# DeltaNet and a multiplicative FFN in one hand-ordered kernel: a new list of steps behind the 130th

## The chip, the cores and the metric

The kernel runs on one core of one Trainium2 chip. The metric is the device time of one execution in microseconds (us), lower is better. The time before is a median of three runs. Engines are named as the profile names them: PE is TensorE's matmul, PEld its weight load, DVE is VectorE, ACT is ScalarE, POOL is GpSimd, SP is SyncE, which issues nearly all DMAs.

## What is computed

```python
# q, k, v: (4, 8, 768, 48), beta: (4, 8, 768); all float32
k_n = k / (np.linalg.norm(k, axis=-1, keepdims=True) + 1e-06)
for t in range(S):
    y[:, :, t] = np.einsum('bhd,bhde->bhe', q[:, :, t], state)
    v_old = np.einsum('bhde,bhd->bhe', state, kt)
    state = state + bt[:, :, :, None] * np.einsum('bhd,bhe->bhde', kt, vt - v_old)
x = y.transpose(0, 2, 1, 3).reshape(3072, 384)
a, b = x @ w1, x @ w2          # w1, w2: (384, 1024), float64 inputs
out = ((a * b) @ w3) @ w_out   # w3: (1024, 1024), w_out: (1024, 384)
```

The first part is a delta-rule attention over 768 tokens for 32 pairs of batch and head; the second is an FFN whose two branches are multiplied elementwise. The four weights arrive as float64 and are converted on the chip.

## The kernel before

**The work.** The 768 tokens are cut into 12 chunks of 64. For each chunk the kernel builds triangular score matrices, inverts them (two chunks together) and runs a short chain that updates the state; from the chain's results it makes the transposed attention output xT. The FFN works on units of two chunks (u = 0 to 5). w3 and w_out are multiplied together once, ahead of all units ("folds"), so that a unit needs a product with w1, one with w2, the elementwise product, and one product with the folded weight. Strassen-like sums of weights and tokens save some of the products.

**The order.** Each piece of work is a Python generator, and each `yield` ends a step. A string, ORDER, lists 1,458 steps by name; the kernel walks through it and lets the named generator make its next step. The same name stands in the list as often as it has steps. Afterwards every engine's instructions are chained in exactly this order:

```python
for name in ORDER.split():
    step(name)
in_text_order()      # each instruction behind the one before it on its engine
```

So the list fixes, for each engine, what stands behind what; an engine whose next instruction waits does nothing else. Between engines only data and buffers decide.

**Buffers that matter.** `in_turn(pool, shape, tag, n, ...)` hands out n buffers in rotation, in the order of the list. The two PSUM pools are psF with four single banks (tag "f": transposes, folds and FFN products) and psW with two pairs of banks (tag "w": scores, corners, chains, outputs). An inverse that lives in PSUM keeps ("holds") one of the two pairs from its first copy to its last, and all others then share the other pair:

```python
V = two_banks().rearrange("p a (s t) -> p (a s) t", t=BS)
held.add(("w", turns["w"]))
```

**The steps.** In this document "t4#2" is the second time that t4 stands in the list, which is its second step.

- P0 to P35: a piece of a weight. #1 DMA issues (SP, L791), #2 ACT (L799, L800), #3 DVE (L802, L803), #4 POOL (L807). P0 to P7 are w_out, P8 to P23 w3, P24 to P29 w1, P30 to P35 w2.
- t0 to t15: transpose of a w3 piece. #1 PE (L842) into a bank of psF, #2 ACT copy (L845).
- f0 to f7: fold. #1 and #2 PE (L856), #3 ACT (L863).
- g0 to g5: squares of k; POOL products (L285) and DVE reductions (L287) alternate (for g1: #1, #3, #5, #7 POOL, #2, #4, #6, #8 DVE), then ACT. N0 to N5: norms, on DVE.
- p, d: load q and k permuted (SP), transpose them on DVE (L339).
- s0 to s11: scores. #1 PE (L383, L389), #2 DVE (L395), #3 the masked part (DVE L413 in chunks 2 and 3); then the second half likewise.
- u, V0 to V5: layout for the inverse, and the inverse. V1#1 sets a buffer on POOL, V1#2 transposes on DVE, V1#3 and #4 copy into PSUM on ACT (L475), V1#5 to #35 are 31 pairs of DVE instructions (L484, L489; L495, L500 in other forms), V1#36 transposes back.
- e0 to e11: corner of the inverse; in chunks 0 to 3: #1 and #3 ACT (L549), #2 POOL, #4 DVE, #5 PE (L576), #6 ACT (L601), #7 PE (L576), #8 ACT (L621).
- c0 to c11: chain. For c1 and later: #1 PE, #2 DVE, #3 PE, #4 DVE (L687), #5 PE, #6 DVE; c0 starts with what is #3 there. y0 to y11: outputs. #1 PE (L746), #2 ACT into xT (L767), #3 DMAs of 16 rows of xT.
- b and a00 to a07: FFN products of unit 0 (PE L876). a, h, i, j with two digits: those of the later units (PE L995). T, W, S, G: sums of weights and tokens on POOL. o, x: the last product (PE L1105) and the results.

Of the kernel before, what the change touches and what calls it, by code (L numbers as in the profile page):

```python
# [40 lines left out]
beta K0 K0 K0 k1 K1 P10 P11 P12 P3 P12 g0 g0 Q0 P10 g0 g0 g0 g0 g0 P8 Q0 Q0 Q0 K1 K1 K1 Q0 K1 P3  # L41
N0 P9 k2 P8 P8 P10 s0 P8 N0 g1 s0 s0 s0 s0 s0 s0 u0 q1 P2 Q1 P9 p2 P2 P12 P12 P9 Q1 g1 Q1 Q1 P2
u0 g1 Q1 d2 d2 u0 P5 P1 t0 t0 t5 t5 P9 t2 t2 P4 P6 s1 s1 P5 P5 P2 s1 P1 s1 s1 s1 u1 g1 P1 u1 u1
t4 V0 V0 P5 V0 V0 P4 t10 P7 P4 t3 t3 V0 V0 P1 f1 P6 P6 t4 V0 P7 V0 V0 t10 t1 P14 P7 P4 V0 f0 V0
P6 P16 P16 V0 V0 P7 t1 s0 P19 P19 P19 P19 V0 f1 P17 k3 p2 v1 V0 V0 P14 P14 P14 V0 f2 P17 f2 f0 V0
f2 P15 v0 P20 f1 t11 f0 P17 P17 f5 V0 V0 P16 t11 P16 t8 P15 V1 V0 t8 f5 t9 V0 V0 t6 P15 V0 n0 n0
f5 V0 V0 V0 V0 t9 P20 P20 V0 t6 P22 P22 P22 f4 P23 P23 V0 f4 f4 P21 P21 P15 t7 t7 V0 s1 V0 V0 V0
V0 g1 d2 d2 P22 f3 f3 P24 P20 g1 g1 p3 g1 P26 p3 P30 e0 e0 e0 t12 t14 e1 e1 g1 f3 e0 e0 d3 d3 N1
s2 s2 s2 P23 P23 t12 e0 f6 e0 p4 s2 P24 e1 e1 t14 s2 e0 P24 s2 P25 c0 P26 f7 u2 P30 P24 c0 e1 e1
P21 P21 d3 d3 y0 y0 P26 P26 P31 t15 t13 s3 s3 s3 s3 s3 s3 t13 c0 n1 n1 P32 t15 u2 u2 u3 c0 P30 f7  # L50
e1 P25 P25 P31 P31 P27 c1 c1 u3 u3 f6 e1 c1 V1 V1 V1 y0 P31 f6 f7 P25 P27 V1 V1 V1 V1 P30 b1 c1
N1 b1 v2 P32 V1 V1 P27 V1 s1 y1 y1 b2 V1 d4 V1 V1 P28 P29 P32 b2 P27 V2 V1 V1 V1 y1 b3 V1 V1 P28
P28 b0 P32 c1 b2 b2 b3 b1 b1 b0 P29 P29 b0 P29 a03 a03 a02 V1 b0 V1 d4 V1 V1 a01 V1 P28 V1 V1 a02
V1 P35 a01 a00 a00 n2 n2 a04 a04 b7 P33 P33 a05 a05 P34 P34 a01 a07 b7 V1 b4 b5 V1 V1 V1 V1 k4
a01 a07 k5 b5 b3 g2 b4 V1 V1 P35 V1 V1 g2 c1 e2 e2 e2 e2 a06 a06 g2 e3 e3 e3 b3 g2 g2 a00 a02 a02
p4 v3 d4 d4 p5 a00 e2 P34 c2 c2 e2 P34 e2 b6 P35 P35 e2 c2 c2 e3 a03 g2 g2 P33 b6 y2 g2 P33 g2 d5
d5 p5 c2 c2 y2 a04 e3 s4 N2 e3 s4 a03 s4 b6 b6 s4 s4 s4 s4 T e3 T T d5 n3 d5 a04 e3 b4 b4 b7 s5
n3 k6 g3 u4 s5 s5 s5 s5 s5 s5 b5 b7 b5 a05 T c3 c3 a06 a05 a06 u5 V2 p6 g3 a07 a07 c3 c3 g3 S0 S0
S0 V2 g3 V2 V2 N2 oD0 y3 y3 V2 V2 W oA0 S0 S0 V2 V2 S0 S0 S0 c3 v5 n5 V2 V2 S0 S0 S0 S0 V2 v4 oB0
V2 V2 V2 xA0 V2 V2 xB0 V2 V2 oA0 S0 S0 S0 n4 oB0 xA0 d6 y3 k7 xA0 V2 n4 oC0 V2 V2 V2 a10 xB0 S0  # L60
V2 V2 xC0 G1 V2 xD0 a10 a10 V2 oC0 a10 a10 d6 xC0 xC0 xC0 xD0 V2 V2 i10 V2 h10 c3 c4 V2 V2 j10 V2
V2 V2 a10 h10 i10 a12 V2 V2 h10 W W a12 p6 V2 a12 a12 j12 e4 g3 g3 h10 c4 a12 h10 a12 h12 d6 d6
s5 i12 e4 e4 e4 i10 h12 h12 g3 g3 p7 g3 e4 e4 h12 N3 s4 h12 a11 a11 a11 s6 s6 i12 i12 e5 c4 j11
s6 c4 y4 y4 c4 e5 d7 d7 h11 c4 c5 a11 p7 e5 s6 a11 a11 h11 i11 i11 n5 c5 d7 d7 N3 a13 h11 h11 e5
W e5 s7 e5 a13 s7 s7 s7 s7 s7 s7 a13 a13 s6 s6 c5 i11 k8 u7 u6 g4 g4 g4 S1 V3 V3 c5 p8 h11 s6 g4
h13 a13 j13 a13 i13 h13 i13 i13 S1 h13 V3 h13 h13 V3 V3 y5 V3 V3 V3 V3 V3 V3 d8 V3 V3 V3 y5 oC1
oA1 S1 oD1 S1 S1 V3 V3 S1 xA1 c5 oA1 xA1 oB1 v6 y5 v7 a20 a20 V3 xA1 V3 V3 V3 d8 G2 V3 V3 xB1 n6
V3 V3 V3 V3 oB1 xB1 xC1 S1 j20 k9 V3 xD1 V3 V3 V3 V3 S1 oC1 a20 a20 p8 xC1 V3 xC1 h20 V3 xD1 xC1
V3 V3 V3 V3 a20 a20 i20 h20 a22 h20 g4 c5 g4 g4 g4 a22 V3 j22 d8 h20 h20 e6 i20 g4 a22 d8 a22 h22
a22 a22 i22 e6 V4 e6 c6 i20 h22 e6 i22 h22 n7 h22 e6 e6 a21 a21 a21 n6 c6 p9 c6 s8 i22 N4 h21 h22  # L70
i21 a21 s8 a21 s6 c6 y6 s8 s8 j21 s8 v8 a21 h21 i21 y6 d9 d9 e7 p9 e7 s8 s8 e7 e7 s7 h21 h21 i21
h21 a23 c6 c6 e7 a23 i23 a23 n8 n8 d9 e7 S2 N4 d9 a23 s9 s9 s9 s9 s9 n7 s9 k10 s9 u8 g5 a23 a23
c7 c7 h23 h23 i23 i23 c7 c7 g5 u9 h23 h23 V4 V4 V4 j23 h23 S2 g5 g5 V4 V4 V4 V4 p10 v9 V4 y7 y7
V4 V4 oA2 V4 V4 d10 V4 y7 V4 V4 S2 oD2 S2 d10 xA2 V4 S2 S2 oB2 oC2 V4 c7 xB2 V4 V4 V4 V4 oB2 xB2
xC2 xD2 p10 V4 V4 V4 oA2 V4 V4 a30 a30 G3 a30 a30 S2 S2 oC2 k11 V4 xC2 j30 s9 V4 xD2 xC2 V4 V4 V4
V4 V4 V4 xA2 xA2 xC2 g5 a30 h30 a30 i30 a32 h30 V4 V4 V4 e8 h30 i30 c7 a32 j32 h30 h30 g5 a32 a32
i32 g5 g5 d10 d10 i30 a32 a32 e8 h32 h32 i32 p11 e8 e8 a31 a31 c8 e8 s8 c8 g5 a31 j31 e8 c8 n9 c8
h32 h32 h32 y8 y8 c8 e9 e9 i31 d11 d11 h31 e9 e9 n9 a31 c8 s10 a31 p11 i32 N5 s10 s10 a31 h31 s10
s10 s10 s10 c9 c9 h31 e9 e9 d11 d11 u10 i31 i31 s11 a33 a33 S3 a33 v11 h31 h31 s11 s11 s11 s11
s11 a33 c9 i33 a33 a33 c9 h33 h33 s11 u11 i33 i33 j33 h33 h33 V5 V5 V5 V5 y9 S3 h33 V5 V5 V5 v10  # L80
n10 n10 oA3 S3 S3 V5 V5 oD3 V5 oB3 s10 y9 y9 oC3 V5 V5 S3 S3 V5 V5 V5 V5 V5 xA3 xB3 V5 V5 n11 V5
V5 oB3 V5 xB3 xD3 xC3 xC3 xD3 oA3 G4 a40 S3 S3 a40 a40 V5 oC3 N5 V5 V5 V5 xA3 a40 a40 xC3 h40 a40
h40 i40 V5 V5 V5 V5 h40 h40 V5 j40 h40 i40 V5 V5 V5 V5 a42 a42 a42 a42 i42 h42 a42 j42 xA3 V5 V5
a42 i40 h42 i42 h42 h42 a41 a41 a41 a41 h41 a41 V5 e10 e10 e10 e10 h42 n11 a41 i42 h41 i41 i41
i41 h41 e10 e11 h41 e10 c9 j41 a43 a43 a43 S4 c9 e11 e11 e11 h41 c10 c10 h43 c10 a43 e11 j43 xC3
a43 c10 a43 i43 h43 i43 i43 h43 h43 e11 h43 c10 c10 y10 y10 c11 s11 oD4 c11 c11 c11 oA4 xA4 y11
S4 S4 S4 oB4 oA4 y11 y11 S4 S4 S4 xA4 xB4 oB4 xB4 oC4 xC4 xA4 a50 xC4 S4 oC4 xC4 xD4 xD4 a50 G5
a50 h50 a50 a50 i50 a50 h50 i50 i50 h50 h50 j50 h50 a52 a52 a52 a52 i52 a52 a52 h52 a51 h52 i52
j52 h52 h52 h52 i51 a51 a51 a51 h51 i52 S5 a51 a51 h51 i51 j51 h51 h51 i51 a53 a53 a53 a53 h53
a53 a53 h53 j53 h51 h53 h53 h53 i53 i53 i53 xC4 o5 x5 o5 S5 S5 o5 o5 x5 S5 S5 S5 S5 o5 x5 x5 o5  # L90
x5 x5 x5 x5 x5 x5 S5 o5 x5 x5 x5 x5
"""


# [1200 lines left out]
```

## Time and profile before

| | us |
|---|---|
| median of 3 runs (lowest, highest) | 554.49 (554.44, 555.08) |
| the profiled execution's own time | 556.72 |
| its span, first to last instruction | 555.0 |
| PE busy | 523.2 (94%) |
| PEld busy | 449.2 (81%) |
| DVE busy | 390.5 (70%) |
| ACT busy | 188.1 (34%) |
| POOL busy | 257.8 (46%) |
| mean granted TensorE clock | 0.991 |

The profile is one execution. "Busy" is the time in which an engine executes an instruction of the program. A matmul's end is modelled, so a stretch in which PE is busy throughout can hide short waits. In rows of the timeline the columns are start, duration (both us), engine, line, operation, output and inputs, number of instructions, and in brackets the idle time ahead and what ended it. In rows of waits the columns are the waiting engine and line, what it waited for, the total in us, how often, and the longest.

### The profile page before, as it was taken

What the parts mean: (1) busy time and instruction counts of PE and PEld (TensorE: products, weight loads), DVE (VectorE), ACT (ScalarE), POOL (GpSimd) and SP (SyncE); (2) the same over time, 40 slices, a digit from 0 to 9 for tenths busy, and PEclk for the clock granted to TensorE, in tenths of its full rate; (3) what the DMA queues carried; (4) which work ended last, traced back from release to release, by engine and by line L of the source; (5) the groups of instructions that cost most, each with busy time, mean ns of one, the idle gap of its engine ahead of it and who ended that gap; (6) DMA issues with size and microseconds to landing.
All of it is one profiled execution on the core that took longest, in us unless ns stands there. A gap on an engine that the chain in (4) does not pass through costs nothing.

```text
span 555.0 us, 19886 instructions
## 1 busy us (share of the span) xinstructions
PE 523.2 (94%) x8540; PEld 449.2 (81%) x8540; DVE 390.5 (70%) x850; ACT 188.1 (34%) x393; POOL 257.8 (46%) x278
## 2 busy tenths in 40 slices
PE   2587999999999999999999999999999999999997
PEld 2473666688778988889987889988899888998897
DVE  3989999899976878659976579858587644124332
ACT  4788288954542112332021530123231121300000
POOL 8585553723658970455443255510382212341141
PEclk9987999999999999999999999999999999999999
DMA  8977976579356445345553564353421220020001
GB/s 248 240 184 195 219 161 127 124 167 146 60 81 116 87 110 81 60 97 92 99 110 61 79 113 65 108 78 47 96 51 44 59 55 4 8 67 1 0 1 57
DMA packets 197688, 52.64 MB, mean 95 GB/s; under 512 B 185345, under 2 KB 191489, under 8 KB 197601
## 3 DMA queue, kind: packets, MB, share of 16 engines
q1 hardware_dynamic: 193408, 50.59, 44.1%
q8 instruction: 67, 1.10, 0.8%
q10 hardware_dynamic: 4192, 0.79, 0.8%
q14 instruction: 21, 0.16, 0.1%
HBM read 41.25 MB, written 8.91 MB: 90 GB/s over the span
## 4 chain that ended last, share of the span: by engine, by line
PE 68%; DVE 11%; DMA 8%; ACT 7%; SPq 2%; issue 2%; POOL 1%; DVEq 0%; POOLq 0%; ACTq 0%
PE ps_f L995 32%; PE ps_f L1105 16%; PE ps_w L647 5%; DMA raw<-in_moe_w_dram 5%; PE ps_w L746 4%; PE ps_w L576 2%; PE ps_w L383 2%; PE ps_f L876 2%; PE ps_w L389 2%; PE ps_f L856 2%; DVE tb L484 1%; DVE tb L495 1%; ACT xT L767 1%; DVE ps_w L489 1%; DVE ps_w L500 1%
## 5 line engine op out<-in xcount | busy, mean ns | idle before, releaser
L1003 DVE TENSOR_TENSOR ab<-ab,ps_f 128x512 f32<-128x512 f32 x80 | 54.6, 683 | 58.1 <-PE ps_f L995 57.5
L1076 POOL TENSOR_TENSOR ab<-ab 128x512 f32<-128x512 f32 (+1 forms) x56 | 61.3, 1118 | 41.0 <-PE ps_f L1105 29.5
L995 PE MATMUL ps_f<-xT,w1s 128*128 128x256 f32 x320 | 78.5, 382 | 0.0
L1042 POOL TENSOR_TENSOR ab<-ab,late 128x512 f32<-128x512 f32 x19 | 24.1, 1270 | 108.2 <-DVE ab L1003 108.2
L995 PEld LDWEIGHTS ps_f<-xT,w1s 128*128 128x128 f32 x320 | 59.9, 190 | 7.9
L1105 PE MATMUL ps_f<-w,ab 128*128 128x192 f32 x376 | 65.6, 329 | 0.0
L1105 PEld LDWEIGHTS ps_f<-w,ab 128*128 128x128 f32 x376 | 61.3, 190 | 1.3 <-issue 0.7
L856 PE MATMUL ps_f<-w2s,w3T 128*128 128x384 f32 x128 | 46.3, 514 | 3.4 <-ACT w3T L845 3.4
L409 POOL TENSOR_TENSOR PT<-PT,smask 128x512 f32<-128x512 f32 x20 | 25.7, 1285 | 51.3 <-ACT PT L407 51.3
L1105 PE MATMUL ps_f<-room,ab 128*128 128x192 f32 x272 | 47.3, 328 | 0.0
L500 DVE TENSOR_TENSOR ps_w<-ps_w,tb 128x31 f32<-128x31 f32 (+15 forms) x124 | 43.3, 349 | 4.3
L767 ACT COPY xT<-ps_w 48x256 f32<-48x256 f32 x96 | 30.4, 365 | 45.2 <-PE ps_w L746 44.7
L495 DVE TENSOR_TENSOR tb<-ps_w,Ub 128x31 f32<-128x31 f32 (+15 forms) x124 | 42.0, 338 | 4.1 <-DMA Ub<-Ud 0.5
L1105 PEld LDWEIGHTS ps_f<-room,ab 128*128 128x128 f32 x272 | 44.3, 190 | 0.6 <-issue 0.3
L1011 ACT COPY ab<-ps_f 128x512 f32<-128x512 f32 x20 | 11.7, 586 | 94.9 <-PE ps_f L995 94.8
L995 PE MATMUL ps_f<-xT,room 128*128 128x256 f32 x160 | 41.2, 385 | 0.0
L856 PEld LDWEIGHTS ps_f<-w2s,w3T 128*128 128x128 f32 x128 | 24.7, 200 | 20.0 <-issue 5.8
L995 PE MATMUL ps_f<-xT,w2s 128*128 128x256 f32 x160 | 40.1, 381 | 0.0
L995 PE MATMUL ps_f<-x_room,w2s 128*128 128x256 f32 x160 | 38.9, 386 | 0.0
L995 PEld LDWEIGHTS ps_f<-x_room,w2s 128*128 128x128 f32 x160 | 29.5, 190 | 5.1 <-DVE late L1003 1.0
L807 POOL TENSOR_TENSOR w<-w,raw 128x512 uint32<-128x512 uint32 x16 | 21.2, 1327 | 26.8 <-DMA raw<-in_moe_w_dram 7.6
L995 PEld LDWEIGHTS ps_f<-xT,room 128*128 128x128 f32 x160 | 29.6, 190 | 4.7 <-DVE osb L1135 0.6
(146 smaller groups left out, 1024.2 us busy)
## 6 DMA issues: line engine op xcount, KB each, us to landing
raw<-in_moe_w_dram SPq DMA_DIRECT2D x16, 512.0 KB, 5.6
vtok<-in_v_dram SPq DMA_DIRECT2D x24, 192.0 KB, 4.2
raw<-in_moe_w_dram SPq DMA_DIRECT2D x24, 192.0 KB, 3.9
out_dram<-osb SPq DMA_DIRECT2D x46, 96.0 KB, 1.7
ktok<-in_k_dram SPq DMA_DIRECT2D x44, 96.0 KB, 3.1
raw<-in_moe_w_out_dram SPq DMA_DIRECT2D x8, 384.0 KB, 3.2
perm<-in_k_dram SPq DMA_DIRECT2D x40, 64.0 KB, 3.0
perm<-in_q_dram SPq DMA_DIRECT2D x32, 64.0 KB, 2.5
```

Source lines behind the costliest of these rows:

```text
L409: pool.tensor_tensor(out=PT, in0=PT, in1=smask[:].unsqueeze(1).to_broadcast([P, H, C]), op=ALU.mult)
L495: dve.tensor_tensor(out=tv, in0=V[:, 0 : s + 1, s : s + 1].to_broadcast([P, s + 1, n]), in1=U[:, s, s + 1 : BS].unsqueeze(1).to_broadcast( ...
L500: dve.tensor_tensor(out=o, in0=o, in1=tv, op=ALU.subtract)
L647: pe.matmul(out(ps, r, h, z), lhsT=lhs(r, h, z), rhs=rhs(r, h, z), start=True, stop=True,)
L746: i = pe.matmul(region(h, z, r), lhsT=lhs, rhs=rhs, start=part[n] not in part[:n], stop=part[n] not in part[n + 1 :],)
L767: act.copy(out=xT[f, p:NP:2, b : b + NR, cc, :].rearrange("p a r t -> p r a t"), in_=pyv[f, z, b : b + NR],)
L856: pe.matmul(ps[:, 0:DM], lhsT=w3Ts[jc, kc // 4][:, kc % 4 * P : kc % 4 * P + P], rhs=wo[:, kc], start=(i == 0), stop=(i == KF - 1),)
L995: pe.matmul(acc[name][:, n * i : n * i + n], lhsT=ws[b][:, P * i : P * i + P], rhs=xs[x], start=new and k == 0 and i == 0, stop=k == len(t ...
L1003: dve.tensor_tensor(out=o_, in0=x, in1=acc[name], op=ALU.add)
L1042: eng.tensor_tensor(out=Z1, in0=Z1, in1=late, op=ALU.mult)
L1076: pool.tensor_tensor(out=o_, in0=x_, in1=y_, op=op)
L1105: pe.matmul(ps[b][:, b, :], lhsT=block(u, HF * f + i, z)[:, P * b : P * b + P], rhs=ws_[w][:, i], start=first and i == 0 and (b == 0 or n ...
```

## The change

The ORDER string is replaced from the 130th step on. The first 129 steps are the same, and the new list holds the same 1,458 steps, each as often as before. It is a new list for the steps behind the 130th, each candidate judged by five draws of landing times and durations. Steps stand on average 8 places from where they stood. Nothing else in the kernel changes. The lists' parts that are spoken of below:

```diff
-t4 V0 V0 P5 V0 V0 P4 t10 P7 P4 t3 t3 V0 V0 P1 f1 P6 P6 t4 V0 P7 V0 V0 t10 t1 P14 P7 P4 V0 f0 V0
-P6 P16 P16 V0 V0 P7 t1 s0 P19 P19 P19 P19 V0 f1 P17 k3 p2 v1 V0 V0 P14 P14 P14 V0 f2 P17 f2 f0 V0
 ...
-f5 V0 V0 V0 V0 t9 P20 P20 V0 t6 P22 P22 P22 f4 P23 P23 V0 f4 f4 P21 P21 P15 t7 t7 V0 s1 V0 V0 V0
-V0 g1 d2 d2 P22 f3 f3 P24 P20 g1 g1 p3 g1 P26 p3 P30 e0 e0 e0 t12 t14 e1 e1 g1 f3 e0 e0 d3 d3 N1
-s2 s2 s2 P23 P23 t12 e0 f6 e0 p4 s2 P24 e1 e1 t14 s2 e0 P24 s2 P25 c0 P26 f7 u2 P30 P24 c0 e1 e1
-P21 P21 d3 d3 y0 y0 P26 P26 P31 t15 t13 s3 s3 s3 s3 s3 s3 t13 c0 n1 n1 P32 t15 u2 u2 u3 c0 P30 f7
-e1 P25 P25 P31 P31 P27 c1 c1 u3 u3 f6 e1 c1 V1 V1 V1 y0 P31 f6 f7 P25 P27 V1 V1 V1 V1 P30 b1 c1
-N1 b1 v2 P32 V1 V1 P27 V1 s1 y1 y1 b2 V1 d4 V1 V1 P28 P29 P32 b2 P27 V2 V1 V1 V1 y1 b3 V1 V1 P28
 ...
-d5 p5 c2 c2 y2 a04 e3 s4 N2 e3 s4 a03 s4 b6 b6 s4 s4 s4 s4 T e3 T T d5 n3 d5 a04 e3 b4 b4 b7 s5
-n3 k6 g3 u4 s5 s5 s5 s5 s5 s5 b5 b7 b5 a05 T c3 c3 a06 a05 a06 u5 V2 p6 g3 a07 a07 c3 c3 g3 S0 S0
 ...
-W e5 s7 e5 a13 s7 s7 s7 s7 s7 s7 a13 a13 s6 s6 c5 i11 k8 u7 u6 g4 g4 g4 S1 V3 V3 c5 p8 h11 s6 g4
+t4 V0 V0 P5 V0 V0 P4 t10 P7 t3 t3 f1 P6 P4 P1 V0 V0 t10 P4 P6 P6 V0 V0 P7 P7 t4 V0 t1 V0 V0 f2 P7
+f2 P14 P14 P16 P16 P19 P16 P19 f0 V0 V0 P17 P17 P16 k3 t1 P19 f1 f1 V0 V0 V0 f0 f0 P19 t11 g1 g1
 ...
+t6 f3 P17 t7 V0 t9 V0 V0 V0 P20 P20 P22 P23 P20 P21 P24 t8 f3 P22 p3 V0 P22 n0 n0 f4 t9 f4 P22 n1
+g1 g1 P20 f3 t12 V0 V0 P21 V0 V0 t14 e0 e0 e0 d2 d2 e0 e0 e1 e1 f4 t12 P24 P23 N1 P24 P24 s2 P26
+s2 s2 f6 t14 d3 d3 e0 e0 e0 P23 P26 n1 s2 s2 s2 f7 e1 P23 t15 p3 d3 e1 d3 s0 c0 e1 c0 P26 e1 t15
+P21 u2 s3 s3 y0 y0 s3 s3 f7 s3 s3 P30 c0 e1 P21 u2 p4 P30 P30 P25 V1 t13 u3 u3 c0 c1 u3 u2 P26
+P31 P32 P27 P25 P25 P25 f7 t13 f6 V1 c1 P31 P31 e1 V1 V1 V1 V1 V1 P30 P32 V2 c1 c1 f6 V1 V1 P32
+s1 y1 P31 V1 P27 y0 y1 v2 b1 P28 P27 P27 b2 V1 b2 V1 V1 d4 b0 P32 b0 b0 c1 b1 V1 d4 V1 V1 V1 V1
 ...
+a04 g2 T g2 a03 e3 g2 e3 c2 N2 N2 a04 p5 b4 b4 S0 s4 s4 k6 s4 s4 s4 g3 s4 b7 s4 b6 u4 e3 e3 d5 d5
+b6 s5 s5 n3 n3 s5 s5 s5 s5 s5 b7 g3 T T c3 c3 a07 g3 u5 V2 b5 V2 c3 b5 c3 a05 a07 a05 a06 T g3 y3
 ...
+y4 y4 S1 c4 e5 e5 d7 d7 p7 h11 e5 h12 c4 a11 c5 c5 a11 a11 i11 h11 e5 h11 d7 d7 e5 k8 g4 h11 e5
+a13 i11 s7 s7 s7 s7 s7 s7 a13 a13 i11 s6 s6 h11 s6 u7 h13 a13 a13 a13 h13 i13 h13 h13 s7 V3 g4 s6
```

What this does on the engines at the places spoken of below, in the order in which each engine meets the steps:

```
ACT  before  t3#2 P6#2 t4#2 P7#2 t10#2 P16#2 t1#2
ACT  after   t3#2 P6#2 t10#2 P7#2 t4#2 P14#2 P16#2
PE   before  e0#5 s2#1 f6#1 e0#7 s2#4 c0#1 f7#1 e1#5 y0#1 t15#1 t13#1 s3#1 s3#4 c0#3 f7#2 e1#7 c1#1 f6#2 c1#3 b1#1 y1#1 b2#1
PE   after   e0#5 s2#1 f6#1 e0#7 s2#4 f7#1 t15#1 c0#1 e1#5 s3#1 y0#1 s3#4 f7#2 c0#3 e1#7 t13#1 c1#1 f6#2 c1#3 y1#1 b1#1 b2#1
ACT  before  e0#1 e0#3 e1#1 g1#9 f3#3 t12#2 e0#6 P24#2 e1#3 t14#2 e0#8 P26#2 u2#1 P30#2 e1#6 y0#2
ACT  after   e0#1 e0#3 e1#1 f4#3 t12#2 P24#2 P23#2 t14#2 e0#6 e0#8 P26#2 e1#3 e1#6 t15#2 u2#1 y0#2 P30#2
```

## The prediction

> **What bounds the kernel now.** I read the engines' shares, then two stages side by side, then what TensorE (PE) waits for in the first of them, then the timeline at the waits. The first fence is from the profile's page, the second from the table of busy time by stretch (engines in the order PE, PEld, DVE, ACT, POOL; then the granted clock, DMA share and GB/s), the third from PE's waits from 45 to 160 us.
>
> ```profile
> PE 523.2 (94%) x8540; PEld 449.2 (81%) x8540; DVE 390.5 (70%) x850; ACT 188.1 (34%) x393; POOL 257.8 (46%) x278
> PE   2587999999999999999999999999999999999997
> PE 68%; DVE 11%; DMA 8%; ACT 7%; SPq 2%; issue 2%; POOL 1%; DVEq 0%; POOLq 0%; ACTq 0%
> ```
>
> ```profile
> 45.00:160.00 115.00, 109.00 (x1894) 80.83 (x1898) 106.12 (x253) 74.83 (x147) 56.20 (x57) 0.97 0.73 148
> 160.00:552.00 392.00, 388.94 (x6161) 347.05 (x6160) 250.47 (x540) 81.57 (x190) 167.57 (x176) 1.00 0.34 66
> ```
>
> ```profile
> PE ps_f L856 <- ACT w3T L845: 3.4, 2, 3.1
> PE ps_w L576 <- ACT late L601: 1.0, 1, 1.0
> PE ps_w L383 <- ACT xT L767: 0.8, 1, 0.8
> PE ps_w L576 <- ACT xT L767: 0.7, 1, 0.7
> PE ps_w L746 <- DVE X L687: 0.5, 1, 0.5
> ```
>
> Behind 160 us PE idles 3 of 392 us: the end is PE's work plus its waits. From 45 to 160 us PE is idle 6 us and VectorE (DVE) 9 us of 115; the two take turns. As no work is added or removed, only waits can change: about 6 us are there to be won between 45 and 160 us, under 3 us behind. A new list can add more than that.
>
> The steps have no times of their own in a page; I matched the trace's instructions with the list, engine by engine in order, so "c1#1 104.1" is where that step starts in the trace. For the changed list I carry each engine forward by hand from the steps' measured durations, only where a step's predecessors change.
>
> **Part by part.** The first 129 steps are kept. SyncE's (SP's) order hardly changes up to 200 us, so the weights land as before.
>
> *The transposes at 45 us.* The timeline there:
>
> ```profile
> 45.33 0.56 ACT L845 COPY w3T<-ps_f 128x512 f32<-128x512 f32 x1
> 46.68 0.57 ACT L845 COPY w3T<-ps_f 128x512 f32<-128x512 f32 x1
> 47.31 1.12 PE L842 MATMUL ps_f<-ident,w 128*128 128x128 f32 x4 [0.39 <-ACT w3T L845]
> 48.06 0.58 ACT L845 COPY w3T<-ps_f 128x512 f32<-128x512 f32 x1
> 48.69 1.65 PE L856 MATMUL ps_f<-w2s,w3T 128*128 128x384 f32 x2 [0.27 <-ACT w3T L845]
> ```
>
> The three copies are t3#2, t4#2 and t10#2. t1#1 takes the PSUM bank that t4 leaves (four in turn: t4, t10, t3, f1, t1), so it starts as t4#2 ends. The new list puts t10#2 (0.58) and P7#2 (1.13) ahead of t4#2: 45.9 + P6#2 1.0 + 0.55 + 1.1 + 0.55 = 49.1 instead of 47.25. Its four transposes take 0.9 at the clock of that place, and the next fold starts at 50.0 instead of 48.7. The clock decides what remains:
>
> ```profile
> 43.79:47.20 3.41, 0.89 (x2) 0.30 (x2) 3.13 (x10) 3.36 (x8) 2.16 (x3) 1.00 0.52 175
> 47.20:50.62 3.42, 3.04 (x7) 1.89 (x8) 3.18 (x11) 2.36 (x6) 1.01 (x1) 0.50 0.90 298
> 50.62:54.03 3.41, 3.41 (x7) 1.74 (x6) 3.17 (x10) 2.99 (x6) 2.24 (x2) 0.50 1.07 251
> 54.03:57.44 3.41, 3.41 (x12) 2.08 (x11) 3.21 (x9) 1.41 (x3) 1.29 (x1) 1.00 0.79 101
> ```
>
> After a stretch in which PE ran 0.89 of 3.41 us the clock is 0.5 for two stretches, though PE was busy 3.04 us of the first. If the full clock comes back at 54.03 again, 1.3 us of later start cost half, 0.65; if it comes back later by as much, 1.3; if a whole stretch later, another 1.7. I take 0.65, the bounds are 0.65 and 2.35: t11#1 at 65.0 instead of 64.3. [...]
>
> *The corner at 80 us.* Two reductions of squares (g1#6 0.51, g1#8 0.54) move ahead of the end of inverse V0, which goes from 79.4 to 80.45. ScalarE (ACT) then does e0#1, e0#3, e1#1 (1.17, 1.08, 1.09), f4#3 0.48, t12#2 0.58, P24#2 1.32, P23#2 1.33 and t14#2 0.59 before e0#6 (1.15); neighbours overlap by some 0.08 each, so e0#6 ends at 88.85; before, it ended at 85.1 with only t12#2 ahead. What PE has as cover is s2#1 and f6#1, to 88.0: e0#7 waits 0.9. In return s2#4 no longer waits (0.5): +0.4, s2#4 at 89.5 instead of 88.45.
>
> *The scores at 97 us.* c0#1 now stands behind f7#1, so c0#2 on DVE, and with it s3#1, is late by 0.5; behind c0#2 DVE does P26#3 (1.47) and P21#3 (1.18) before s3#2 and s3#3 (0.69, 0.68), and s3#4 waits for these 1.75. Before, PE waited here 0.35 (ahead of t15), 0.4 (t13 on POOL) and 1.0 (s3#4): 2.25 against 1.75, +0.5, and 0.1 where f7#2 and c0#3 change places: +0.6, c1#1 at 105.8 instead of 104.1.
>
> *Inverse V1 and y1.* This is the largest term. ACT is idle some 2.4 us between e1#3 and e1#6, since e1#5 now stands behind f7#1 and c0#1 on PE (95.6); then come t15#2, u2#1, y0#2 (2.6), P30#2, u3#1, u3#3, u2#3, P25#2, f7#3, t13#2, P31#2, e1#8, V1#3, V1#4: 14.1 us by their rows, so V1#4 ends at 110.95 instead of 108.1, and the DVE loop behind it is 2.85 late. From V1#3 on the inverse holds one of the two PSUM pairs, so c1#3 and y1#1 share the other. The rows before:
>
> ```profile
> 109.07 1.56 PE L876 MATMUL ps_f<-xT,w1s 128*128 128x256 f32 x6
> 110.18 0.95 DVE L687 TENSOR_TENSOR X<-ps_w,wt 128x768 f32<-128x768 f32 x1
> 111.19 0.67 PE L746 MATMUL ps_w<-KQ,S 48*48 48x64 f32 x32 [0.55 <-DVE X L687]
> ```
>
> b1#1 (first row) covered c1#4 (second) for y1#1 (third). Now y1#1 follows c1#3 directly. c1#3 waits for e1#8 until 109.95; c1#4 stands behind V1#5 to #7 (1.5) and ends at 113.4; y1#1 starts at 113.45, a wait of 2.4 against 0.7; b1#1 follows, and b2#1 starts at 117.1 instead of 113.46: +2.0.
>
> *To the end.* b7#1's third matmul needs P29#4, behind the late loop on DVE: some 0.4. e2#5 needs PE and DVE: DVE comes at 145.4 (142.5 + 2.85), PE at 146.5, so PE decides. Then e2#6 no longer stands behind e3#3 on ACT (-0.5), e3#7 stands behind b7#3 and b6#3 (-0.45), but e3#7, s5#1, s5#5, c3#1 stand close on two pairs (+0.4). At 237 us a13#1 comes between e5#5 and s7#1 (-0.5). Two things are costed at nothing: POOL reaches G2 some 8 us later and is done about 3 us before its first reader needs it (if that is gone, the shortfall itself); y7#3's copies stand behind p10#2 on SP and land near 344, a30#1 reads them at 345.8 (each us beyond that costs one).
>
> Sum: 0.65 + 0.4 + 0.6 + 2.0 + 0.4 - 0.55 - 0.5 = 3.0. The profiled execution took 556.72 with a span of 555.0, 2.2 above the median of 554.49; its span would be 558.0, and the median 557.5.
>
> **The rivals.** *ACT keeps up, faster.* If e0#6 is out by 88.0 and V1#4 by 108.5, the new waits vanish and the lost ones stay lost: 0.5 + 1.0 + 0.8 (s2#4, s3#4, t15 and t13) + 0.5 + 0.45 + 0.5 = 3.75, less 0.65: 551.4, with half of it 553. For it: ACT is busy only 74.83 of 115 us in that stage. Against it: its idle time lies where e1#5 is not yet there, and the order fixes that. Chance 0.17.
>
> *Only V1 is in time.* Without the ACT wait for e1#5, the terms 2.0 and 0.4 go: 555.1, within what can be told. Chance 0.12.
>
> *The clock, on top.* Half speed lasts one stretch longer, +1.7: 559.2. [...] Chance 0.15.
>
> That the list isn't followed is hardly possible: every engine's instructions are chained in the text's order.
>
> **How the numbers follow.** The sum has 0.56, so slower by over 0.2% (1.1 us, about what a measurement of this kernel can tell from no change) is 0.56 + 0.15 = 0.71, same 0.12, faster 0.17. The range goes from 552.8, inside the faster case, to 559.8, the clock case with half a us: outside lie some 0.12 and 0.05.
>
> **What the profile would show.** Right: t1's transposes at 49.1; a wait of about 0.9 of L576 on ACT late L601 at 88; PE L746 waiting over 2 us for DVE X L687 near 111 to 113; the copies to ps_w at L475 ending at 111; L1105's first group 2.5 to 3.5 late; equal work on every engine; behind 180 us a constant offset. Wrong: V1#4 ending by 108.5, or y1 starting before 112; or a wait behind 200 us that shifts the offset by over 1 us.

## The result, and the profile after

| | before | new list |
|---|---|---|
| four executions, median | 554.79 us (554.44 to 558.41) | 564.14 us (561.53 to 565.04) |
| ratio of the means | | 1.0146 (95% interval 1.0111 to 1.0181) |
| profiled execution, span | 556.72, 555.0 us | 561.53, 559.8 us |

The change made the kernel slower by some 8 us (8.1 by the means, 9.4 by the medians). The forecast had the side and most of the places right, but less than half of the size: 557.5 us with 559.8 as the upper end. The profiled execution of the new list is the fastest of its four, that of before one of the slower ones, so the pair of traces shows 4.8 us of it only.

From the profile's page after the change: the engines' row of work, and PE's busy share in 40 slices.

```profile
PE 522.7 (93%) x8540; PEld 449.1 (80%) x8540; DVE 391.6 (70%) x850; ACT 188.4 (34%) x393; POOL 256.9 (46%) x278
PE   2577998889999999999999999999989999999997
```

The work is equal on every engine, as nothing was added. The page's chain of work that ended last is followed back only to 107 us here, and to the start in the page before, so the shares of the two chains can't be compared. The table of busy time by stretch, and what PE waited for from 45 to 160 us (total, times, longest):

```profile
45.00:160.00 115.00, 106.17 (x1789) 79.06 (x1790) 103.81 (x238) 73.55 (x145) 55.94 (x58) 0.97 0.69 144
160.00:552.00 392.00, 388.57 (x6239) 345.98 (x6239) 250.66 (x547) 82.47 (x192) 166.49 (x174) 1.00 0.34 66
```

```profile
PE ps_w L746 <- DVE X L687: 2.0, 1, 2.0
PE ps_f L842 <- ACT w3T L845: 1.7, 1, 1.7
PE ps_w L576 <- issue: 1.1, 1, 1.1
PE ps_w L383 <- DVE PT L413: 0.9, 1, 0.9
PE ps_w L383 <- issue: 0.5, 1, 0.5
PE ps_w L746 <- ACT late L601: 0.4, 1, 0.4
```

In the same 115 us PE is busy 2.8 us less. The forecast's y1 wait (L746) and t1 wait (L842) are there. Two rows say "issue", time in which PE waits for nothing that the profile shows. Before had two such rows as well, of 0.3 and 0.2 us; now they are 1.1 and 0.5. The timeline at the first of them, in step e1#5 (L576), and at a larger one in y9#1 (L746, KQ,S):

```profile
92.32 1.15 PE L647 MATMUL ps_w<-vtok,TT 64*64 64x48 f32 x64
93.29 0.73 PE L576 MATMUL ps_w<-T,U 33*33 33x32 f32 x61
95.09 0.22 PE L576 MATMUL ps_w<-T,U 33*33 33x32 f32 x2 [1.07 <-issue]
```

```profile
406.28 1.08 PE L746 MATMUL ps_w<-PT,X 64*48 64x64 f32 x64
407.48 0.64 PE L746 MATMUL ps_w<-KQ,S 48*48 48x64 f32 x26
409.43 0.32 PE L746 MATMUL ps_w<-KQ,S 48*48 48x64 f32 x6 [1.31 <-issue]
```

The same two steps before:

```profile
93.36 0.74 PE L576 MATMUL ps_w<-T,U 33*33 33x32 f32 x63
404.33 0.66 PE L746 MATMUL ps_w<-KQ,S 48*48 48x64 f32 x32
```

With the new list PE stops inside a run of small matmuls that wait for nothing the profile shows, and goes on over a us later. From the start of the last matmul ahead to the start of the next the gaps are 1.26 and 1.53 us; one more, of 0.70, is at 98.9. Before had 0.69 us of this kind at 303.8 and 0.45 at 159.5. The forecast had no term for it.

### The profile page after: what moved, and what is told of

Read it like the earlier page. It is cut to its first block, busy times and chain, and to the rows that moved or that the text cites. A ratio compares the mean times of both kernels' runs of the same rounds, so it can differ in the third digit from the quotient of the medians.

```text
span 559.8 us, 19897 instructions
## 1 busy us (share of the span) xinstructions
PE 522.7 (93%) x8540; PEld 449.1 (80%) x8540; DVE 391.6 (70%) x850; ACT 188.4 (34%) x393; POOL 256.9 (46%) x278
## 4 chain that ended last, share of the span: by engine, by line
PE 74%; DVE 3%; ACT 1%; issue 1%; DMA 1%; POOL 0%; SPq 0%; DVEq 0%; ACTq 0%
PE ps_f L995 35%; PE ps_f L1105 19%; PE ps_w L647 5%; PE ps_f L876 5%; PE ps_w L746 4%; PE ps_w L576 2%; PE ps_w L383 1%; PE ps_w L389 1%; PE ps_w L1105 1%; DMA vtok<-in_v_dram 1%; DVE tb L484 1%; DVE ps_w L489 1%; PE ps_f L856 1%; ACT xT L767 0%; DVE w1s L803 0%
```

## The experiments

Steps are counted in the lists; "index" is the count of PE's records in the trace (matmuls, weight loads and its sequencer's) from the first. Each group ran on one chip beside the old list ("before"), whose median was 555.0 to 556.0 us. Behind each median stand the ratio to the old list, by the means, and its 95% interval.

**Where is it lost?** The new list again, and three lists that are joined from a stretch of one and the remaining steps in the other's order:

```
again     new list, unchanged
x_early   new[:606] + the rest in the old order     (joint at 181 us)
x_late    old[:606] + the rest in the new order
x_corner  old[:264] + the rest in the new order     (joint at 83 us)
```

> The new list once more, to see what varies between executions. In the profiled execution (span 559.8) 3.3 us of the loss stand by oA0#1 at 181 us and 1.5 us come behind; three others were 563.1 to 563.3 with a lower mean clock (.973 to .978 against .984). Waits only: all executions within 1.5 us of 561.5, the same waits at the same places. Clock: executions part by whole stretches of half speed of 3.41 us (1.7 us each), 561.5, 563.2, 564.9, with half speed 17, 20.5 or more us long. Instruction supply: TensorE idles over 0.5 us in the middle of a step with nothing named as its cause (as for 1.3 us in y9#1 at 407.9), at places that differ between two profiled executions.

> The new list up to 181 us (its first 606 steps), behind it the old one; one step differs at the joint. Waits only: the 3.3 us of 45 to 181 us stay, the 1.5 behind go: 557.9 to 558.5. Clock, lost in the idle time of 42 to 48 us: as much lost as with the whole new list but for the 1.5, 560 to 563, mean clock .973 to .984. A loss spread over the later list: under 556.

> The old list up to 181 us, the new one behind. Waits only: before plus 1.5, 556.0 to 556.5. Clock, lost early: the same 556, with the mean clock of the old list (.99) in every execution. If the later list costs more than the one profiled execution showed (instruction supply, waits that move): 557 to 559.

> The old list up to 83 us (264 steps: transposes and folds as before, so TensorE's idle time from 42 to 48 us is the old one), the new one behind. In the profiled pair the two stood level at 83 us (e0#5 at 82.97 in both). Waits only: no gain, 560.5 to 564 like the new list. Clock, lost in that idle time: the slower executions vanish, 559 to 560.5 with a mean clock of .99 in all. My forecast's sum (0.65 for t1 and clock) would give 0.65 less than the new list.

Measured, against 555.44 of before: again 562.88 (ratio 1.0142, 1.0108 to 1.0176), x_early 562.72 (1.0124, 1.0100 to 1.0147), x_late 557.98 (1.0038, 1.0023 to 1.0054), x_corner 562.53 (1.0121, 1.0094 to 1.0148). So the loss is not made by half clock behind the idle time from 42 to 48 us: x_corner has the old steps there and is no faster by what can be told. Ahead of 181 us lies the larger part, and some 2 us behind. x_early is no clean half: in its trace PE waits 1.7 us, up to 199.7, for POOL (xT L981), which neither list alone has. x_late's trace is the fastest of its twelve executions (555.36) and does not show its median.

The second trace of the new list has the gaps of e1#5 (1.55) and y9#1 (1.54) at the same instructions, so they do not move from one execution to the next, as I had thought possible. It also has half clock where the first had none. The table shows the trace of again in the clock's own stretches of 3.41 us: PE's busy time first, then the other engines', the clock, DMA share and GB/s:

```profile
90.07:93.48 3.41, 3.41 (x103) 2.46 (x102) 3.01 (x6) 1.08 (x2) 3.15 (x4) 1.00 0.89 138
93.48:96.89 3.41, 1.71 (x106) 1.46 (x92) 3.31 (x6) 1.16 (x3) 0.24 (x2) 1.00 0.68 130
96.89:100.31 3.42, 2.50 (x80) 2.29 (x84) 1.08 (x2) 2.91 (x7) 3.24 (x4) 0.50 0.52 150
100.31:103.72 3.41, 3.41 (x45) 2.42 (x38) 1.87 (x3) 3.36 (x7) 1.18 (x2) 0.50 0.94 219
103.72:107.13 3.41, 3.41 (x135) 2.40 (x133) 2.43 (x3) 3.35 (x5) 1.37 (x2) 1.00 0.29 85
```

The stretch with e1#5's gap has PE busy for 1.71 us, and the next two run at half speed.

**What are the gaps?** In these first traces each lies at index 193 of 256, and ends 1.2 to 1.5 us after a transfer of 16 KB in the instruction queue (q8 in the DMA view). If PE runs out of instructions there, moving its whole stream of instructions against these places must move the gaps:

```
         ps = bank([P, NCH, NR * H])
+        for _ in range(4):            # 32 in new_p128 and old_p128
+            pe.matmul(
+                ps[0:32, 0, :], lhsT=ident[0:32, 0:32], rhs=ident[0:32, 0:16],
+                start=True, stop=True,
+            )
         for c in range(NCH):
             pe.transpose(
```

> The new list with 4 small matmuls more (16 instructions on TensorE) in the step beta, at 11 us, where TensorE waits 3 us for a load anyway; nothing else is touched. In five profiles, of both lists, TensorE idles for 0.4 to 1.8 us inside a step with no releaser, and where its small matmuls stand (not the folds at half clock) each such gap lies at instruction 193 of 256 of TensorE's stream and ends 1.2 to 1.5 us after a 16 KB transfer of the instruction queue. Theory instruction supply: 16 instructions more move every step against these boundaries. Between two boundaries the new list has 1.93 us of its own work before e1#5's gap at 93.8 and 3.49 before y9#1's at 407.9; moved by 16 these become 4 us or more, so both gaps vanish (1.3 to 1.8 and 1.5 us), gaps remain only at index 193 of 256 counted anew: 2 to 4 us faster than the new list, 559 to 561. Theory plain waits: 16 short instructions more in idle time change nothing, 562 to 564, the gaps stay in e1#5 and y9#1.

> The new list with 32 small matmuls more (128 instructions) at the same place. Supply: the gaps of e1#5 and y9#1 move or vanish, but from the trace's times of the steps 18 stretches of 256 instructions behind 87 us would now last under 4.2 us (20 as it stands, but shorter ones: their sum lacks 24 us of 4.2 each against 15), so new gaps come at other steps, again all at index 193 of 256: no faster than the new list, up to 4 us slower, 562 to 567. Plain waits: 562 to 564, gaps where they were.

> The old list with the same 128 instructions more. Supply: by the same count (22 us lacking against 13) 1 to 5 us slower than the old list, 556 to 560, with gaps at index 193 of 256 that the old list has not. Plain waits: 554 to 556, and no new gaps.

> The old list once more, for its trace. The profiled execution of before was 1 to 1.5 us above the median of its kernel. If that was early (x_late, with the same first 606 steps, stood 2.1 us earlier from 62 us on), this trace stands 1 to 2 us earlier than the first at t11#1 (64.33) and keeps that to the end, and the new list's loss up to e1#5 is 1 to 2 us larger than the first pair showed; if not, t11#1 is at 64.3.

Measured, against 555.58: new_p16 561.38 (1.0104, 1.0085 to 1.0123), new_p128 571.48 (1.0292, 1.0265 to 1.0319), old_p128 567.34 (1.0209, 1.0177 to 1.0240). 128 short instructions in over 3 us of idle time at the start cost the old list 11.8 us and the new one some 8, both more than I expected, and as much as the change under study or more. With 16 the gaps of e1#5 and y9#1 are gone, as expected, and two of 1.0 come at 297 and 383 us. The distance to the old list falls by some 2 us only, from 7.4 to 5.8 by the medians (expected 2 to 4), and the intervals of again and new_p16 touch. The whole of e1#5's small matmuls in new_p16, in one run:

```profile
93.70 0.76 PE L576 MATMUL ps_w<-T,U 33*33 33x32 f32 x64
```

A gap of new_p128, in a step that has none in the new list:

```profile
157.27 0.86 PE L647 MATMUL ps_w<-X,ktok 64*64 64x48 f32 x48
159.54 0.43 PE L647 MATMUL ps_w<-X,ktok 64*64 64x48 f32 x16 [1.42 <-issue]
```

Over all 17 traces of this study, behind 60 us and outside half clock, PE has 44 gaps over 0.45 us inside its small matmuls that the profile puts down to nothing. All 44 are at index 193 of 256, and they end 1.2 to 1.6 us (median 1.4) after a 16 KB transfer has landed. That they are waits for instructions is shown by this and by the moved streams. The 4 and 4.2 us that the expectations of the moved lists count with were my estimate: the 44 gaps came with 1.9 to 4.8 us of PE's work from one such place to the next, and no run shows a limit at 4.2.

The trace of old_again shows that the first trace of before was a late one. Its span is 552.8 us; it is 1.5 us ahead of the first trace at t11#1 (62.82 against 64.33) and 2.2 at the end. It stands near the median of before and has no such gap, so I measure the new list against it below.

**What makes them long?** In dma_moved two groups of loads move on SyncE alone. dma_b1 also puts b1#1 back ahead of y1#1, and dma_b1_t13 also puts t13#2 earlier on ScalarE:

```
dma_moved    -... u2 p4 P30 P30 P25 V1 ...      +... u2 P30 P30 P25 V1 ...
             -... P27 y0 y1 v2 b1 ...           +... P27 y0 p4 y1 v2 b1 ...
             -... V5 V5 v11 V5 V5 S3 ...        +... V5 V5 V5 V5 S3 ...
             -... xD3 y9 G4 ...                 +... xD3 y9 v11 G4 ...
dma_b1       -... s1 y1 P31 V1 P27 y0 p4 y1 v2 b1 ...
             +... s1 y0 b1 y1 P31 V1 P27 p4 y1 v2 ...
dma_b1_t13   -... u3 u2 P26 ... P25 f7 t13 f6 ...
             +... u3 t13 u2 P26 ... P25 f7 f6 ...
```

> The new list with two groups of loads moved on SyncE's queue alone, TensorE's order and instruction count as in the new list: p4#1 (8 loads in small packets, 89.3 to 92.9) goes behind y0#3 (105.8), v11#1 (two loads of 192 KB at 402.4) behind y9#3 (411.8). In the new list the 16 KB transfer that ends e1#5's gap starts at 92.54, as p4#1 is out, and the one that ends y9#1's at 406.68, as a burst of 403.0 to 406.6 drains (V5#2's 512 KB and v11#1). Theory A, these transfers wait behind the loads: both start 1 to 3 us earlier, e1#5's gap (1.3 to 1.8) falls to under 0.5 and y9#1's (1.5) by 0.8 or more; with it the half clock behind 90 us is rarer: 557.5 to 560.5. Theory B, they start late for another reason: the gaps stay within 0.4 of what they were, 561.5 to 563.5.

> dma_moved, and y0#3 and b1#1 ahead of y1#1, so that b1#1's 1.56 us stand in y1#1's wait for c1#4, as in the old list. My term for V1 and y1 was 2.0, of which 1.3 to 1.6 is this place: y1#1's wait falls from 2.2 to about 0.7, b2#1 starts 1.5 earlier, and 0.8 to 1.5 of it is left at 181 us: 0.8 to 1.5 below dma_moved. Rival, VectorE's late inverse decides anyway (its loop starts with V1#4 as before): y1#1's wait falls and the time returns at b7#1 or e2#5, under 0.4 below dma_moved.

> dma_b1, and t13#2 ahead of u2#3 on ScalarE (ahead of P25#2 and f7#3): f6#2 no longer waits 1.0 for it at 106.4. If that wait counts: c1#1 to y1#1 1.0 earlier less what f7#3 (0.5 later) costs, 0.3 to 0.8 below dma_b1. If V1#4 and c1#4 set this stretch: y1#1 where it was, within 0.3 of dma_b1.

Measured, against 554.99: dma_moved 562.99 (1.0142, 1.0128 to 1.0157), dma_b1 563.36 (1.0161, 1.0135 to 1.0186), dma_b1_t13 565.38 (1.0184, 1.0170 to 1.0197). Half of theory A holds, the gap in y9#1; the time did not follow, as 562.99 lies in the range of theory B. In y9#1 the gap is gone in all three; dma_moved:

```profile
408.18 1.07 PE L746 MATMUL ps_w<-PT,X 64*48 64x64 f32 x64
409.37 0.67 PE L746 MATMUL ps_w<-KQ,S 48*48 48x64 f32 x32
```

There the transfer starts 0.74 us after PE has passed the index 193 before (406.31 to 407.05), where it took 2.27 in the first trace of the new list (404.41 to 406.68, as the burst of loads drained). In e1#5 the gap grew:

```profile
93.33 0.73 PE L576 MATMUL ps_w<-T,U 33*33 33x32 f32 x61
96.43 0.22 PE L576 MATMUL ps_w<-T,U 33*33 33x32 f32 x2 [2.37 <-issue]
```

P25's loads moved up into p4's place, and the transfer starts at 93.70 instead of 92.54. By the first trace's figures e1#5 could not be served in time: PE passes the 256 instructions ahead of it in 1.93 us, while 0.64 from the one place to the start of the transfer, 1.17 for it and 1.4 from its landing to the end of the gap make 3.2. But the start is not fixed: in x_corner's trace the transfer starts 0.12 us ahead of the place, and the gap in e1#5 is only 0.40. That the p4 loads made this gap was not borne out; as other loads took their place, no run shows e1#5 with a quiet queue ahead of it.

dma_b1 takes y1#1's wait away and gains nothing in the median; its trace has half clock from 109.7 to 113.2, so what the place is worth alone stays open. dma_b1_t13 came out 2 us slower by the median, where I expected a gain, though the two intervals overlap. f6#2's wait is gone, but in the trace PE then waits 1.9 us for e1#8's TT (L621) and 1.4 for a load of k, and has half clock twice, from 97.5 and from 114.6 us.

**Which stretch, and how much of it is plain waiting?** The stretch from 83 to 121 us alone in the other order, with and without the 16 instructions:

```
mid_old       new[:264], old order up to old[:389], rest new
mid_new       old[:264], new order up to new[:389], rest old
mid_new_p16   mid_new with the 4 matmuls in beta
old_p16       old list with the 4 matmuls in beta
```

> The new list with the steps between the 264th and the 389th (83 to 121 us: scores, V1, y1, b2) in the old list's order. If most of the loss is made there (5 of 7.4 us, waits, e1#5's gap and half clock together): 557 to 559.5, no gap in e1#5, no half clock between 85 and 125. If it is made by what comes before (the transposes at 45 us) or behind: 561 or more.

> The converse: the old list, with these steps in the new order. Same theory: 558 to 561, e1#5's gap of 1.3 to 2 us and in some executions half clock behind 90. My forecast's terms alone (scores 0.6, V1 and y1 2.0) would give 557.5 to 558.

> mid_new with 16 TensorE instructions more in the step beta. If instruction supply makes the difference between my terms and what mid_new costs: e1#5's gap is gone and it stands 1 to 2.5 us below mid_new, 2 to 3 above old_p16 (the waits of my sum). If it is all waits: within 0.7 of mid_new.

> The control: the old list with these 16 instructions. By the count of short stretches the old list is as well off as without (12.7 us lacking against 13.0): 554 to 556.5, gaps, if any, at other steps and at index 193 of 256.

Measured, against 556.02: mid_old 560.70 (1.0071, 1.0052 to 1.0090), mid_new 561.81 (1.0095, 1.0061 to 1.0129), mid_new_p16 561.40 (1.0090, 1.0057 to 1.0122), old_p16 557.64 (1.0032, 1.0013 to 1.0052). The stretch costs the old list 5.8 us. Giving it back to the new one returns 2.7, and the 560.70 lies between the two ranges expected; y9#1's gap (1.54 in mid_old's trace) and more stay.

Two of these did not come out as expected. The control: 16 instructions cost the old list 1.6, where I expected next to nothing. Its trace has gaps of 0.5 and 0.6 us at 160 and 294 us, less than the 1.6; counting short stretches foresaw a loss with 128, not one with 16. And mid_new_p16 is only 0.4 below mid_new, where I expected 1 to 2.5 by instruction supply and under 0.7 by plain waits. Its trace has no gap in e1#5, and has half clock all the same, behind a stretch in which PE was busy 1.47 us because y1#1 waits:

```profile
110.24:113.65 3.41, 1.47 (x103) 1.35 (x99) 3.14 (x11) 2.83 (x5) 3.35 (x4) 1.00 0.39 74
113.65:117.07 3.42, 3.32 (x75) 2.78 (x66) 3.28 (x9) 1.20 (x4) 0.63 (x2) 0.50 1.03 249
```

new_p16 has the same at the same place. So plain waits bring half clock as well, and taking e1#5's gap away gains little alone. Against its control, old_p16, mid_new_p16 loses 3.8 (expected 2 to 3).

Two differences of step starts tell the parts of this stretch apart (us; the range over the traces). Left out are the two lists with 128 instructions and x_corner (half clock from 89.8 without the gap, 17.8 in the first row), and in the second row also dma_b1 and dma_b1_t13, whose order differs there:

| from to | old order | new, no gap in it, full clock | with e1#5's gap | with half clock |
|---|---|---|---|---|
| s2#4 to c1#1 (scores) | 15.4 to 16.0 | 16.0 | 17.5 | 18.7 to 20.0 (and the gap) |
| c1#1 to b2#1 (V1, y1) | 9.3 to 10.0 | 10.7 to 12.0 | | 12.1 to 13.3 |

## Why the prediction was right or wrong

The forecast's running sum at some steps, and how late the two traces of the new list are against old_again:

| start of step | forecast | first trace | again |
|---|---|---|---|
| s2#4 (88 us) | +1.05 | +0.7 | +0.65 |
| c1#1 (104) | +1.65 | +2.75 | +4.95 |
| b2#1 (114) | +3.65 | +4.8 | +6.15 |
| oA0#1 (179) | +3.5 | +4.6 | +5.65 |
| oA1#1 (255) | +3.0 | +5.6 | +6.8 |
| oA3#1 (405) | +3.0 | +7.1 | +8.3 |
| end | +3.0 | +7.0 | +7.9 |

*The transposes* (0.65). t1#1 starts at 47.99, not 49.1: ScalarE came there 0.7 earlier, and its steps overlap more than I added up. The forecast also misread two rows of before here and one below: P7#2 took 1.02 us (not 1.13), t1's transposes 1.12 (not 0.9), and y1#1 waited 0.55 (not 0.7). Over the traces, eight with the old steps up to 83 us and nine with the new reach e0#7 at 86.7 and 87.2 on average: about 0.5, within a scatter of over 1 either way. The row of 47.04 after the change, with PE busy 2.47 us, was followed by half clock, and the next, with 3.41, by full clock. Half clock lasted 6.83 us here in both traces of the first pair, so the rival of a longer one did not come, and neither trace shows its 1.7 at this place.

*The corner* (+0.4) did not occur: g1#6 ran already at 57.5 us, V0 ended at 78.5, not 80.45, ScalarE had e0#6 out at 87.23, and e0#7 started without a wait. The lost wait of s2#4 was a gain of 0.4 in the first pair.

*The scores* (0.6) come out at 0 to 0.6 where e1#5 has no gap: 16.0 against 15.4 to 16.0 us. In those traces s3#4 waits 1.3 us for s3#2 and s3#3, by the way forecast (1.75). With the gap the stretch takes 1.5 to 2 us more, and 3 to 4 more where half clock follows.

*V1 and y1* (2.0) came at the size forecast, in part by luck. The copies of V1#3 and V1#4, c1#4's operation and y1#1:

```profile
109.72 1.21 ACT L475 COPY ps_w<-Vb 128x512 f32<-128x512 f32 x2
112.38 0.95 DVE L687 TENSOR_TENSOR X<-ps_w,wt 128x768 f32<-128x768 f32 x1
113.38 0.67 PE L746 MATMUL ps_w<-KQ,S 48*48 48x64 f32 x32 [2.00 <-DVE X L687]
```

V1#4 ends at 110.93 (forecast 110.95), y1#1 starts at 113.38 (113.45), b2#1 at 117.05 (117.1) and e2#5 at 146.05 (146.5). The forecast counted from the late trace of before, and s2#4 starts 1.5 us ahead of it, at 88.01 and not 89.5; the gap in e1#5 made up for that. In new_p16, without the gap, V1#4 ends at 110.1. From c1#1 to b2#1 the first trace takes 2.07 us longer than old_again. Of this 1.3 is y1#1's wait, the way forecast (2.00 against 0.72), and 0.8 is f6#2's wait for t13#2, which the forecast had not walked. In `again`, where f6#2 does not wait, the stretch is 1.2 longer. So the place is worth 1.2 to 1.3 in these two traces.

*Behind 181 us* I had a constant offset, and named a wait that shifts it by over 1 us as what would prove me wrong. There is one: y9#1 to oA3#1 takes 3.88 us against 2.27, nearly all of it the gap. Another 1.0 to 1.1 is lost from 181 to 259 us (0.9 on average over the traces with each order). The gain of 0.5 by a13#1 ahead of s7#1 is there: s7#1 takes 0.9 us and not 1.5. What is lost is 0.1 to 0.25 us in each of many steps whose neighbours on PE changed, alike in all traces: a13#1 takes 0.86 us in the 7 traces with the old order there and 1.06 in the 10 with the new, y4#1 2.16 and 2.36. PE doesn't idle more there. Why a step takes longer beside another neighbour stays open.

So the step that failed is the first one, "only waits can change", with the sum built on it. That sum has only waits of one step for another, and puts three things at nothing. The first is PE's waits for its own instructions: 1.3 to 1.8 us in e1#5, 0.7 in s3#4 in some traces, 1.5 in y9#1. The second is half clock behind 60 us, 3.4 to 6.8 us long, at 97 us in `again` and between 90 and 121 us in 9 of the 11 traces with the new order from 83 to 121 us. The third is the 0.9 us of changed neighbours on PE. Waits of steps for steps cost about 3 us as summed, though not all where I put them.

The gaps and the half clock can't be priced apart. Without the gaps of e1#5 and y9#1, new_p16 was some 2 us nearer to the old list; without e1#5's, mid_new_p16 gained 0.4, with half clock behind a plain wait. I had the clock as a rival "on top", with 1.7 us; it came, but at 97 or 114 us and not at 50. The range ended too low for want of these mechanisms, though the trace of before held a row of the first (0.69 us at 303.8), which I left out.

In the first trace of the new list the instruction queue q8 moved 67 transfers of 16,384 bytes, and PE has 17,229 records, 67.3 times 256; the gaps lie at one index of 256. The old list as it stands lost little to them (no gap over 0.45 us in old_again, two in the first trace). At the 44 gaps PE ran through 256 instructions in 1.9 to 4.8 us.

No version here beats the old list, and none of the parts points to one.

## What to carry to other kernels

An order on an engine with many small matmuls also decides which step is running at the places where PE waited for its own instructions here, at index 193 of 256 in all 44 gaps: look for "issue" gaps inside a step, and check that they lie at one index. Gaps over 0.45 us came here with 1.9 to 4.8 us of PE's work from one such place to the next, but not at every place with so little: where the transfer started ahead of the first place, 2.2 us were enough. So look at when the transfer starts, and keep bursts of loads away from it: y9#1's gap went as its burst did.

An edit that adds instructions ahead of such a stretch can move the time by itself; here 16 or 128 instructions moved three lists by 1.6 to 11.8 us up, and two by 0.4 and some 2 down. So compare orders only over several executions. Idle time of PE can also cost a second time, by the clock: where PE was busy under 2.2 us of a stretch of 3.41, half clock followed in 14 of 33 cases here.

## What the runs showed of the hardware

Sixteen instructions more on PE, in idle time, cost the old list 1.6 us and gained the new one some 2 (the intervals with and without them still touch); 128 cost 11.8 and some 8. At the 44 gaps, the 16 KB transfer started from 0.2 us before to 2.7 us after PE passed the same index 256 records earlier, took 0.9 to 1.5 us, and the gap ended 1.2 to 1.6 us after that. What releases the transfer is open: in the old list (the first trace) the one ahead of y9#1 started at 397.43, 4 us before PE passed that place (401.49).

The clock was granted in stretches of 3.41 us whose edges lie elsewhere from one execution to the next (one at 88.57 us in old_again, at 90.07 in again). Behind 60 us, all 8 stretches with PE busy under 1.8 us were followed by half clock, 6 of 25 with 1.8 to 2.2, and none of 32 with more (up to 2.6). In the three traces of the old list that are not moved by 128 instructions the least is 2.22, and none was followed by half clock; with the new list the stretch from 93.48 in `again` has 1.71 and was, the one from 111.89 in the first trace has 1.81 and was not. For the way back these traces show no such difference: half-clock stretches with PE busy 2.74 and 2.96 us were followed by full clock, others with 3.2 to 3.41 were not.
